# Two long convolutions' last products: own PSUM banks for their third and fourth stage, spare places for late loads and shuffles, additions shared out anew, statistics held back

## The chip, the core and the metric

The kernel runs on one core of a Trainium2 chip. Its engines are TensorE (PE: matmuls), ScalarE (ACT), VectorE (DVE), GpSimd (POOL) and SyncE (SP, which issues DMAs). Each engine takes its instructions in program order; semaphores tie the engines together. PSUM has banks of 2 KB for each of 128 partitions; matmuls write there. The metric is the device time of one execution in microseconds (us).

## The reference

```python
x = A_x                                          # 1 x 2048 x 640, f32
x = x + attention(layernorm(x))                  # 32 heads of 20
x = x + conv(layernorm(x))                       # state space, below
x = x + attention(layernorm(x))
x = x + conv(layernorm(x))

def conv(u, ...):
    K = 2 * real(einsum("dn,dnl->dl", C, exp(A * dt * pos)))
    y = irfft(rfft(u.T, 2 * L) * rfft(K, 2 * L), 2 * L)[:, :L]
    return y.T + u * D_skip
```

The convolution of 640 channels over 2048 positions is done as a Fourier transform, a product with the transformed kernel K, and the transform back.

## The kernel before

The four layers run one after the other: attention 1 (to about 1240 us of the profile), convolution 1 (1259 to 1404), attention 2 (to about 2446, then its output projection), convolution 2 (2493 to 2641, then the last output's DMA). "Conv 1" and "conv 2" stand for the two calls of `ssm`; only the second has `last=True`.

`ssm` is one loop over n = 0 to 54. Channels are in 5 blocks b of 128 (NCT), positions in 16 tiles of 128 (NI). Each block needs eight steps of every stage, so 40 products in all (NQ), and one n holds, in this order: at every fourth n the four spectra `psx` of four products (`sets`, 48 matmuls into four banks F0 to F3); a transpose `pst` (`stage2a`); the loads of product n-2 (`factors`); the sum `x<-x,psy` of the round before; product n-4 (`product`); the first stage of the next block (`stage1`, none from n=32 on); the bn_stats of the round before, for the next layer's norm, in conv 1 only; third stage n-6 (`stage3`: 8 matmuls into `psv`, two ACT copies `v<-psv`); fourth stage n-14 (`stage4`: 8 matmuls into `psy`, of block b and pair i2 of position tiles). `psy` needs the whole `v` of its block. Product k is named by its number 0 to 39, `psy(3,2)` is block 3, i2=2.

One product is four instructions: DVE's shuffle `t<-psx`, DVE's `ka<-psx,ka`, POOL's `kb<-t,kb` and POOL's `ka<-ka,kb`; for k=37 and 39 DVE does the last two too (`alone`). `ka` and `kb` are loaded by SP's DMAs, 256 KB each; `kb` has three buffers (pool `s3`), `t` has one (pool `s4`).

`at` writes the order out by hand: on each engine every instruction of the loop stands behind the one that the code gave it before, so the order of the code is the order of the engine. At the seam between conv 1 and attention 2 a scheduler places what isn't tied. Recorded through a helper, most operations have line 78.

Of the eight banks two belong to pool X, four to F, two to pool M. The two of M (tag `mm`) are shared by `psv`, `psy` and some of stage 1 (`psx1`); the allocator gives a new tile one of the two. Attention 2 begins with the norm: rs and nb of four position tiles (`rstd`), xn on ACT, a transpose `pst`, its split xh and xl, weights wb from DMAs b0s and b1s, then the product `pq`.

Of the kernel before, what the change touches and what calls it, by code (L numbers as in the profile page):

```python
# [11 lines left out]
F32 = mybir.dt.float32  # L12
# [9 lines left out]
P = 128  # L22
L = 2048
D = 640
NI = L // P
NCT = D // P
# [61 lines left out]
def mha_s4d_kernel(ctx, tc, x_in, wqkv, wo, lar, aim, cr, ci, ldt, dsk,  # L88
# [19 lines left out]
    def psum(c, **pools):  # L108
        for n, b in pools.items():
            ps_[n] = c.enter_context(tc.tile_pool(name="ps" + n, bufs=b, space=PSUM))  # L110

    def pst(pool, *a, **k):
        return ps_[pool].tile(*a, **k)
# [7 lines left out]
    ks = dram.tile([2, D, L], F16, name="ks")  # L121
# [65 lines left out]
    last = [None]  # L187
# [1207 lines left out]
    def ssm(x, uh, ul, consts, last):  # L1395
# [19 lines left out]
        with ExitStack() as c:  # L1415
            c1 = c.enter_context(tc.tile_pool(name="s1", bufs=1))
            if last:
                cx = c.enter_context(tc.tile_pool(name="sx", bufs=2))
            c4 = c.enter_context(tc.tile_pool(name="s4", bufs=1))
            c2 = c.enter_context(tc.tile_pool(name="s2", bufs=2))  # L1420
            c3 = c.enter_context(tc.tile_pool(name="s3", bufs=3))
            if not last:
                cx = c2
# [5 lines left out]
            def mm(*a, **k):  # L1429
                at("pe", te.matmul(*a, **k))  # L1430
# [3 lines left out]
            def stage1(b, x1, i2):  # L1434
                bs = slice(b * P, b * P + P)
                spare = b == 1 and i2 in (1, 3, 5) or not b and i2 % 4 > 1 and not last
                pool, tag = ("M", "mm") if spare else ("X", "X")
                ps = pst(pool, [P, 2, 2, P], F32, tag=tag, name="psx1")
                for i in range(2):
                    s = 2 * i2 + i  # L1440
                    for r in range(2):
                        for n, (e, m) in enumerate(((0, uh), (0, ul), (1, uh))):
                            mm(ps[:, r, i, :], e1[:, e, s, r, :], m[:, s, bs], start=(n == 0), stop=(n == 2))
                src = ps.rearrange("p r i (c g) -> p (r i) c g", c=4)
                at("act", se.copy(by_channel(x1[0], i2), src))
                return lambda: at("dve", ve.tensor_sub(by_channel(x1[1], i2), src, by_channel(x1[0], i2)))
# [17 lines left out]

            def factors(m, ch):
                ka = c4.tile([P, 512], F32, bufs=5, name="ka")
                kb = c3.tile([P, 512], F32, name="kb")
                for t, src in ((ka, kha), (kb, khb)):
                    at("sp", sy.dma_start(t.rearrange("p (q k) -> p q k", k=P), src[m][:, ch]))
                return ka, kb  # L1470

            def product(px, ka, kb, alone):
                t2 = c4.tile([P, 512], F32, name="t2")
                at("dve", ve.stream_shuffle(t2, px, SWAP))
                at("dve", ve.tensor_mul(ka, px, ka))
                for f, *a in (("tensor_mul", kb, t2, kb), ("tensor_add", ka, ka, kb)):
                    if alone:
                        at("dve", getattr(ve, f)(*a))
                    else:
                        at("pool", getattr(ge, f)(*a))  # L1480
                return ka

            def stage3(v, t, ch, t1):
                pv = pst("M", [P, 4, 2, NI, 4], F32, tag="mm", name="psv")
                for q in range(4):
                    mm(pv[:, q].rearrange("p r i g -> p (r i g)"), t1[:, q * P:q * P + P], fa, start=True, stop=True)
                for r in range(2):
                    at("act", se.copy(v[:, r, :, ch, 16 * t:16 * t + 16].rearrange("p i (q g) -> p i q g", g=4),
                                      pv[:, :, r].rearrange("p q i g -> p i q g")))

            def stage4(b, v, i2):
                bs, s2 = slice(b * P, b * P + P), slice(2 * i2, 2 * i2 + 2)
                py = pst("M", [P, 2, P], F32, tag="mm", name="psy")
                for i in range(2):
                    for r in range(2):
                        mm(py[:, i, :], eb[:, 2 * i2 + i, r, :], v[:, r, 2 * i2 + i].rearrange("p c g -> p (c g)"),
                           start=(r == 0), stop=(r == 1))

                def add():
                    at("dve", ve.tensor_add(x[:, s2, bs], x[:, s2, bs], py))  # L1500

                def after():
                    if last:
                        if i2 % 2:
                            s4 = slice(2 * i2 - 2, 2 * i2 + 2)
                            at("sp", sy.dma_start(ov[:, s4, bs], x[:, s4, bs]))
                    elif b < NCT - 1:
                        for i in (2 * i2, 2 * i2 + 1):
                            at("dve", ve.bn_stats(st[:, i, b, :], x[:, i, bs]))
                    elif i2 == 1:  # L1510
                        final(0)
                return add, after
# [4 lines left out]
            x1 = new_x1()  # L1517
            for i2 in range(8):
                stage1(0, x1, i2)()
            ks, t1s, vs = {}, {}, {}  # L1520
            NQ = 8 * NCT
            nxt, px = None, None
            sums = None
            for n in range(NQ + 15):
                b, q = divmod(n, 8)
                if n % 4 == 0 and 4 <= n <= NQ:
                    px = sets(xt)
                if n < NQ:
                    if q == 0 and b:
                        x1 = nxt  # L1530
                    if n % 4 == 0:
                        xt = c4.tile([P, 2, 4, 4, P], F16, name="xt")
                    stage2a(x1, q, xt)
                if 2 <= n < NQ + 2:
                    ks[n - 2] = factors(*divmod(n - 2, 4))
                if sums:
                    sums[0]()
                if 4 <= n < NQ + 4:
                    t1s[n - 4] = product(px[n % 4], *ks.pop(n - 4), n > NQ and n % 2 == 1)
                if n < NQ and b + 1 < NCT:  # L1540
                    if q == 0:
                        nxt = new_x1()
                    stage1(b + 1, nxt, q)()
                if sums:
                    sums[1]()
                    sums = None
                if 6 <= n < NQ + 6:
                    m, ch = divmod(n - 6, 4)
                    if m % 2 == 0 and ch == 0:
                        vs[m // 2] = c2.tile([P, 2, NI, 4, 32], F32, name="v")  # L1550
                    stage3(vs[m // 2], m % 2, ch, t1s.pop(n - 6))
                if 14 <= n < NQ + 14:
                    bb, i2 = divmod(n - 14, 8)
                    sums = stage4(bb, vs[bb], i2)
# [93 lines left out]
    def seq(x, general):  # L1648

        stats = None  # L1650
        for n in range(0, len(parts), 2):
            with ExitStack() as c:
# [8 lines left out]
                c3 = ExitStack()  # L1661
# [35 lines left out]
                if not general:  # L1697
                    wc.close()
                c3.close()
                psum(c, M=2, F=1)  # L1700
                end = n + 2 >= len(parts)
                stats = ssm(x, uh, ul, consts, end)
            if early:
# [90 lines left out]
```

## Time and profile before

| | us |
|---|---|
| median of 3 runs | 2644.64 |
| lowest, highest | 2643.77, 2650.95 |
| profiled execution, its span | 2647.0 |
| PE busy | 2492.4 (94%) |
| ACT busy | 2344.0 (89%) |
| DVE busy | 1519.5 (57%) |
| POOL busy | 801.7 (30%) |

For the profiled execution the span from its first to its last instruction is the only time given; it is 2.4 us above the median. The mean granted clock of PE is 0.994. In a timeline a row gives the start, the length from first to last instruction of the row, the instructions, and in brackets how long the engine had been idle and what released it. Rows without a bracket followed with no idle time that counts. Matmuls are pipelined, so a group's length overlaps the next one's; the distance of two starts is what a group costs.

### The profile page before, as it was taken

Reading aid. Unit: us, or ns where it says so; the run is one execution under the profiler, and the core shown is the slowest. Engines: PE = TensorE matmul, PEld = TensorE weight load, DVE = VectorE, ACT = ScalarE, POOL = GpSimd, SP = SyncE. Lnnn points to the kernel's source line nnn. Section 1 sums busy time; section 2 is a strip of 40 time slices with the busy share of each in tenths; the row PEclk is TensorE's granted clock in tenths of the full one; section 3 lists DMA queues with packets and bytes.
Section 4 is the critical chain, followed back from the end, with each engine's and each line's share of the span. In section 5 each row is a group of like instructions: output and inputs, shape, how many; then the busy total and the mean of one; then the engine's idle time right before and its main releaser. Section 6 shows DMA issues by size and latency. Waiting matters only on the chain.

```text
span 2647.0 us, 118800 instructions
## 1 busy us (share of the span) xinstructions
PE 2492.4 (94%) x52388; PEld 1409.8 (53%) x52388; DVE 1519.5 (57%) x3430; ACT 2344.0 (89%) x2763; POOL 801.7 (30%) x1230
## 2 busy tenths in 40 slices
PE   6899999999999999899898999999999998999898
PEld 3444444454444444587896544454444443444898
DVE  7587777777765887577786323232232222143875
ACT  7899999999999999655665899999999999999574
POOL 1123333233323332111681122222222223222285
PEclk9999999999999999999999999999999999999999
DMA  6522222322222221654652111121121113222466
GB/s 206 189 53 77 68 74 62 82 65 63 61 54 59 53 63 38 234 206 163 213 173 64 47 53 50 51 60 45 45 66 39 50 34 87 71 66 61 137 190 184
DMA packets 188158, 241.99 MB, mean 91 GB/s; under 512 B 43504, under 2 KB 128816, under 8 KB 186224
## 3 DMA queue, kind: packets, MB, share of 16 engines
q1 hardware_dynamic: 151936, 188.28, 22.6%
q0 software_dynamic: 35696, 46.01, 7.4%
q8 instruction: 413, 6.77, 1.1%
q14 instruction: 113, 0.93, 0.1%
HBM read 158.16 MB, written 76.00 MB: 88 GB/s over the span
## 4 chain that ended last, share of the span: by engine, by line
ACT 59%; PE 20%; issue 10%; DVE 3%; DMA 2%; POOL 1%; SPq 0%; ACTq 0%; POOLq 0%; DVEq 0%
ACT pt L78 57%; PE psy L1430 3%; PE pa L903 2%; PE psv L1430 2%; PE po L193 2%; PE psx L1430 2%; PE S L868 2%; PE pst L1452 1%; PE pkx L193 1%; PE pv L586 1%; PE m L620 1%; PE pkt L196 1%; PE pq L773 1%; DMA kb<-khb 1%; DMA kop<-ks 1%
## 5 line engine op out<-in xcount | busy, mean ns | idle before, releaser
L78 ACT ACTIVATE pt<-S 128x1024 f32<-128x1024 f32 x2048 | 1927.7, 1033 | 27.9 <-PE S L868 15.5
L903 PE MATMUL pa<-pt,V 64*32 64x512 f32 x16384 | 1096.9, 589 | 1.4 <-DVE oc L78 1.4
L868 PE MATMUL S<-qop,kop 61*32 61x512 f16 x16384 | 877.2, 380 | 82.7 <-ACT pt L78 67.8
L868 PEld LDWEIGHTS <-kop 61*32 61x32 f16 x16384 | 366.9, 89 | 737.3 <-issue 619.2
L903 PEld LDWEIGHTS pa<-pt,V 64*32 64x32 f32 x16384 | 312.7, 106 | 72.0 <-issue 8.6
L78 POOL DMA_DIRECT2D dn<-oc x248 | 122.7, 501 | 574.2 <-DVE oc L78 574.1
L78 DVE TENSOR_SCALAR qc<-m 128x512 f32<-128x512 f32 (+1 forms) x68 | 46.8, 688 | 312.0 <-PE m L620 312.0
L78 POOL DMA_DIRECT2D db<-dn x248 | 125.4, 512 | 141.5 <-DMA dn<-dr 136.9
L78 POOL DMA_DIRECT2D ot<-oc x256 | 130.5, 517 | 88.4 <-DVE oc L78 55.5
L620 PE MATMUL m<-xl,wh 64*32 64x512 f16 x2560 | 143.8, 376 | 0.3 <-issue 0.3
L620 PE MATMUL m<-xh,wh 64*32 64x512 f16 x2560 | 144.1, 378 | 0.0
L620 PE MATMUL m<-xh,wl 64*32 64x512 f16 x2560 | 143.8, 377 | 0.0
L78 DVE COPY oc<-pa 128x512 f32<-128x512 f32 x64 | 44.2, 690 | 172.9 <-PE pa L903 168.9
L78 ACT COPY xt<-pst 128x1024 f16<-128x1024 f16 x80 | 81.3, 1016 | 60.8 <-PE pst L1452 60.8
L620 PEld LDWEIGHTS <-wh 64*32 64x32 f16 x5120 | 90.3, 93 | 73.3 <-issue 30.8
L78 POOL DMA_DIRECT2D dn<-dr x62 | 34.6, 558 | 287.3 <-DVE dr L78 248.6
L1480 POOL TENSOR_TENSOR kb<-t,kb 128x512 f32<-128x512 f32 x76 | 97.2, 1280 | 65.2 <-DVE t L78 40.8
L78 DVE TENSOR_SCALAR V<-m 128x160 f32<-128x160 f32 x64 | 20.7, 324 | 163.4 <-PE m L586 163.4
L78 DVE TENSOR_TENSOR kb<-ktab 128x512 f32<-128x512 f32 x160 | 106.2, 683 | 0.0
L586 PEld LDWEIGHTS <-xh 128*128 128x128 f16 x960 | 79.7, 98 | 46.7 <-issue 31.4
L1480 POOL TENSOR_TENSOR ka<-ka,kb 128x512 f32<-128x512 f32 x76 | 97.5, 1283 | 6.0
L337 PEld LDWEIGHTS m<-kb,ka 128*32 128x32 f32 x3840 | 60.8, 109 | 71.0 <-issue 52.4
(312 smaller groups left out, 3936.4 us busy)
## 6 DMA issues: line engine op xcount, KB each, us to landing
ka<-kha SPq DMA_DIRECT2D x80, 256.0 KB
kb<-khb SPq DMA_DIRECT2D x80, 256.0 KB
db<-dn POOLq DMA_DIRECT2D x248, 64.0 KB, 3.2
kop<-ks SPq DMA_DIRECT2D x176, 80.0 KB
kpw<-wd POOLq DMA_DIRECT2D x60, 192.0 KB, 3.9
qop<-qs SPq DMA_DIRECT2D x256, 40.0 KB
ot<-oc POOLq DMA_DIRECT2D x256, 40.0 KB, 3.0
kha<-kn SPq DMA_DIRECT2D x20, 512.0 KB
```

Source lines behind the costliest of these rows:

```text
L78: made = f(out, *a, **k)
L193: chain(te.matmul(*a, **k))
L196: chain(te.transpose(*a, **k))
L337: chain(te.matmul(ps[32 * j:32 * j + 32, c8, :], a[n][:, ch, :], b[n][:, dd, :], start=(n == 0), stop=(n == 2), tile_position=(0, 32 * j)))
L586: chain(te.matmul(ps[:, :n], a_[:, ct, sl], m[:, ct, :], start=(k == 0), stop=(k == 14)))
L620: chain(te.matmul(ps[r][32 * t:32 * t + 32, :], a_[rows, ct, 32 * u:32 * u + 32], m[rows, ct, 512 * v:512 * v + 512], start=(k == 0), stop ...
L773: te.matmul(pq, a_[:, ct, :], m[:, ct, sl], start=(n == 0), stop=(n == 14))
L868: chain(te.matmul(S[32 * t:32 * t + 32, 512 * r:512 * r + 512], kt_[rows, kc + 32 * t:kc + 32 * t + 32], qt[rows, :], start=True, stop=Tru ...
L903: chain(te.matmul(pa[r][32 * j:32 * j + 32, :], V[rows, kt, VP * h:VP * h + 32], pts[j // 2][rows, 512 * (j % 2):512 * (j % 2) + 512], sta ...
L1430: at("pe", te.matmul(*a, **k))
L1452: at("pe", te.transpose(pt[:, k, g, :], of_group(x1[k], 4 * q + g), id16))
L1480: at("pool", getattr(ge, f)(*a))
```

## The change

Pool M goes; pools V and Y get one bank each. `psv` lives in V, `psy` in Y, but the `psy` of block 4 with odd i2 in V; the spare `psx1` take V or Y.

From n=34 on the two buffers of the first stage's `x1` are not used any more; they are taken over as `room0`, four places for the shuffled spectra of products 32 to 39, and `room1`, four places for the kb loads of the same products.

POOL's and DVE's shares of products change: k=37 goes back to POOL whole, k=38 goes to DVE whole, and of k=33, 35 and 39 DVE does the addition alone. Of the 16 POOL-kind operations of k=32 to 39 DVE had 4 and has 5.

In conv 1 the bn_stats of the rounds n-1=40 to 45 (block 3, i2 = 2 to 7: 12 instructions) are held and issued one pair a round at n=49 to 54.

```diff
--- before.py
+++ after.py
@@ -1434,8 +1434,8 @@
             def stage1(b, x1, i2):
                 bs = slice(b * P, b * P + P)
                 spare = b == 1 and i2 in (1, 3, 5) or not b and i2 % 4 > 1 and not last
-                pool, tag = ("M", "mm") if spare else ("X", "X")
-                ps = pst(pool, [P, 2, 2, P], F32, tag=tag, name="psx1")
+                pool = ("Y" if b or i2 % 2 else "V") if spare else "X"
+                ps = pst(pool, [P, 2, 2, P], F32, tag=pool, name="psx1")
                 for i in range(2):
                     s = 2 * i2 + i
                     for r in range(2):
@@ -1464,24 +1464,24 @@
 
             def factors(m, ch):
                 ka = c4.tile([P, 512], F32, bufs=5, name="ka")
-                kb = c3.tile([P, 512], F32, name="kb")
+                kb = room[1][:, ch] if m >= 2 * NCT - 2 else c3.tile([P, 512], F32, name="kb")
                 for t, src in ((ka, kha), (kb, khb)):
                     at("sp", sy.dma_start(t.rearrange("p (q k) -> p q k", k=P), src[m][:, ch]))
                 return ka, kb
 
-            def product(px, ka, kb, alone):
-                t2 = c4.tile([P, 512], F32, name="t2")
+            def product(px, ka, kb, k):
+                t2 = room[0][:, k % 4] if k >= NQ - 8 else c4.tile([P, 512], F32, name="t2")
                 at("dve", ve.stream_shuffle(t2, px, SWAP))
                 at("dve", ve.tensor_mul(ka, px, ka))
                 for f, *a in (("tensor_mul", kb, t2, kb), ("tensor_add", ka, ka, kb)):
-                    if alone:
+                    if k == NQ - 2 or f == "tensor_add" and (k == NQ - 1 or k in (NQ - 7, NQ - 5)):
                         at("dve", getattr(ve, f)(*a))
                     else:
                         at("pool", getattr(ge, f)(*a))
                 return ka
 
             def stage3(v, t, ch, t1):
-                pv = pst("M", [P, 4, 2, NI, 4], F32, tag="mm", name="psv")
+                pv = pst("V", [P, 4, 2, NI, 4], F32, tag="V", name="psv")
                 for q in range(4):
                     mm(pv[:, q].rearrange("p r i g -> p (r i g)"), t1[:, q * P:q * P + P], fa, start=True, stop=True)
                 for r in range(2):
@@ -1489,8 +1489,9 @@
                                       pv[:, :, r].rearrange("p q i g -> p i q g")))
 
             def stage4(b, v, i2):
+                pool = "V" if b == NCT - 1 and i2 % 2 else "Y"
                 bs, s2 = slice(b * P, b * P + P), slice(2 * i2, 2 * i2 + 2)
-                py = pst("M", [P, 2, P], F32, tag="mm", name="psy")
+                py = pst(pool, [P, 2, P], F32, tag=pool, name="psy")
                 for i in range(2):
                     for r in range(2):
                         mm(py[:, i, :], eb[:, 2 * i2 + i, r, :], v[:, r, 2 * i2 + i].rearrange("p c g -> p (c g)"),
@@ -1520,9 +1521,11 @@
             ks, t1s, vs = {}, {}, {}
             NQ = 8 * NCT
             nxt, px = None, None
-            sums = None
+            sums, held = None, []
             for n in range(NQ + 15):
                 b, q = divmod(n, 8)
+                if n == NQ - 6:
+                    room = [cx.tile([P, 4, 512], F32, tag=f"x1{k}", name=f"room{k}") for k in range(2)]
                 if n % 4 == 0 and 4 <= n <= NQ:
                     px = sets(xt)
                 if n < NQ:
@@ -1536,14 +1539,16 @@
                 if sums:
                     sums[0]()
                 if 4 <= n < NQ + 4:
-                    t1s[n - 4] = product(px[n % 4], *ks.pop(n - 4), n > NQ and n % 2 == 1)
+                    t1s[n - 4] = product(px[n % 4], *ks.pop(n - 4), n - 4)
                 if n < NQ and b + 1 < NCT:
                     if q == 0:
                         nxt = new_x1()
                     stage1(b + 1, nxt, q)()
                 if sums:
-                    sums[1]()
+                    (held.append if not last and NQ <= n - 1 < NQ + 6 else lambda f: f())(sums[1])
                     sums = None
+                if held and n > NQ + 8:
+                    held.pop(0)()
                 if 6 <= n < NQ + 6:
                     m, ch = divmod(n - 6, 4)
                     if m % 2 == 0 and ch == 0:
@@ -1697,7 +1702,7 @@
                 if not general:
                     wc.close()
                 c3.close()
-                psum(c, M=2, F=1)
+                psum(c, V=1, Y=1, F=1)
                 end = n + 2 >= len(parts)
                 stats = ssm(x, uh, ul, consts, end)
             if early:
```

DVE at the end of conv 1, before: the sum of `psy`, the shuffle, the product and the statistics of k=33 and k=34.

```order
L78 TENSOR_TENSOR x<-x,psy 128x2x128 [waits PE_49]
L78 STREAM_SHUFFLE t_31085<-psx_30984 128x512 [waits Pool_49]
L78 TENSOR_TENSOR ka<-psx_30984,ka 128x512 [waits DMAHW6_49]
L78 BN_STATS st_28889<-x 128x6 [waits DVE_49]
L78 BN_STATS st_28889<-x 128x6
L78 TENSOR_TENSOR x<-x,psy 128x2x128 [waits PE_49]
L78 STREAM_SHUFFLE t_31119<-psx_30985 128x512 [waits Pool_49]
L78 TENSOR_TENSOR ka<-psx_30985,ka 128x512 [waits DMAHW0_49]
L78 BN_STATS st_28889<-x 128x6 [waits DVE_49]
L78 BN_STATS st_28889<-x 128x6
```

DVE at the same place now; `room_30918` is the place of the shuffles, `room_30919` that of the kb loads.

```order
L78 TENSOR_TENSOR x<-x,psy 128x2x128 [waits PE_49]
L78 STREAM_SHUFFLE room_30918<-psx_30987 128x512
L78 TENSOR_TENSOR ka<-psx_30987,ka 128x512 [waits DMAHW6_49]
L78 TENSOR_TENSOR ka<-ka,room_30919 128x512 [waits DMAHW7_49,DVE_49,Pool_49]
L78 BN_STATS st_28892<-x 128x6 x2
L78 TENSOR_TENSOR x<-x,psy 128x2x128 [waits PE_49]
L78 STREAM_SHUFFLE room_30918<-psx_30988 128x512
L78 TENSOR_TENSOR ka<-psx_30988,ka 128x512 [waits DMAHW0_49]
L78 BN_STATS st_28892<-x 128x6 [waits DVE_49]
L78 BN_STATS st_28892<-x 128x6
```

The addition of k=33 has come in ahead of the statistics and of the next sum of `psy`, and it waits for POOL; the shuffles no longer wait for POOL.

POOL at the end of conv 1, products 33 to 36, before.

```order
L1480 TENSOR_TENSOR kb<-t_31051,kb 128x512 [waits DMAHW5_49,DVE_49]
L1480 TENSOR_TENSOR ka<-ka,kb 128x512 [waits DVE_49,DMAHW4_49,PE_49,Pool_49]
L1480 TENSOR_TENSOR kb<-t_31085,kb 128x512 [waits DMAHW7_49,DVE_49]
L1480 TENSOR_TENSOR ka<-ka,kb 128x512 [waits DVE_49,DMAHW6_49,PE_49,Pool_49]
L1480 TENSOR_TENSOR kb<-t_31119,kb 128x512 [waits DMAHW1_49,DVE_49]
L1480 TENSOR_TENSOR ka<-ka,kb 128x512 [waits DVE_49,DMAHW0_49,PE_49,Pool_49]
L1480 TENSOR_TENSOR kb<-t_31154,kb 128x512 [waits DMAHW3_49,DVE_49]
L1480 TENSOR_TENSOR ka<-ka,kb 128x512 [waits DVE_49,DMAHW2_49,PE_49,Pool_49]
```

POOL at the same place now, products 33 to 37.

```order
L1480 TENSOR_TENSOR room_30919<-room_30918,room_30919 128x512 [waits DMAHW5_49,DVE_49]
L1480 TENSOR_TENSOR ka<-ka,room_30919 128x512 [waits DVE_49,DMAHW4_49,PE_49,Pool_49]
L1480 TENSOR_TENSOR room_30919<-room_30918,room_30919 128x512 [waits DMAHW7_49,DVE_49]
L1480 TENSOR_TENSOR room_30919<-room_30918,room_30919 128x512 [waits DMAHW1_49,DVE_49]
L1480 TENSOR_TENSOR ka<-ka,room_30919 128x512 [waits DVE_49,DMAHW0_49,PE_49,Pool_49]
L1480 TENSOR_TENSOR room_30919<-room_30918,room_30919 128x512 [waits DMAHW3_49,DVE_49]
L1480 TENSOR_TENSOR room_30919<-room_30918,room_30919 128x512 [waits DMAHW5_49,DVE_49]
L1480 TENSOR_TENSOR ka<-ka,room_30919 128x512 [waits DVE_49,DMAHW4_49,PE_49,Pool_49]
```

The additions of k=33 and 35 are gone from POOL, so it goes from one kb product to the next one; each of these waits for a shuffle of DVE.

PE at the end of conv 1 before, from `psv` of k=36 and `psy(3,4)` on.

```order
L1430 MATMUL psv<-fa,ka 128x128 [waits PE_49,DMAHW4_49,Activation_49,Pool_49]
L1430 MATMUL psv<-fa,ka 128x128 x3
L1430 MATMUL psy<-v,eb 128x128 [waits PE_49,Activation_49]
L1430 MATMUL psy<-v,eb 128x128 x3
L1430 MATMUL psv<-fa,ka 128x128 [waits DMAHW6_49,DVE_49]
L1430 MATMUL psv<-fa,ka 128x128 x3
L1430 MATMUL psy<-v,eb 128x128 [waits PE_49,Activation_49]
L1430 MATMUL psy<-v,eb 128x128 x3
```

PE at the same place now.

```order
L1430 MATMUL psv<-fa,ka 128x128 [waits PE_49,DMAHW4_49,Activation_49,Pool_49]
L1430 MATMUL psv<-fa,ka 128x128 x3
L1430 MATMUL psy<-v,eb 128x128 [waits DVE_49]
L1430 MATMUL psy<-v,eb 128x128 x3
L1430 MATMUL psv<-fa,ka 128x128 [waits PE_49,DMAHW6_49,Activation_49,Pool_49]
L1430 MATMUL psv<-fa,ka 128x128 x3
L1430 MATMUL psy<-v,eb 128x128 [waits DVE_49]
L1430 MATMUL psy<-v,eb 128x128 x3
```

`psy` waited for ACT, which empties the `psv` just written; it now waits for DVE, which empties the `psy` of the round before.

## Rows read from the trace of the kernel before

**Rows 1.** The page, part 4: the chain that ended last, by engine.
```profile
ACT 59%; PE 20%; issue 10%; DVE 3%; DMA 2%; POOL 1%; SPq 0%; ACTq 0%; POOLq 0%; DVEq 0%
```

**Rows 2.** Timeline, PE, end of conv 1: start us, us, instructions [idle before <-releaser].
```profile
1374.61 1.11 PE L1430 MATMUL psv<-fa,ka 128*128 128x128 f32 x8
1375.56 1.06 PE L1430 MATMUL psy<-v,eb 128*128 128x128 f32 x8
...
1385.99 1.16 PE L1430 MATMUL psv<-fa,ka 128*128 128x128 f32 x8
1387.89 1.16 PE L1430 MATMUL psy<-v,eb 128*128 128x128 f32 x8 [0.73 <-ACT v L78]
...
1395.35 8.43 PE L1430 MATMUL psy<-v,eb 128*128 128x128 f32 x72
```

**Rows 3.** Timeline, ACT, end of conv 1.
```profile
1387.19 0.65 ACT L78 COPY v<-psv 128x256 f32<-128x256 f32 x2 [1.31 <-PE psv L1430]
```

**Rows 4.** Timeline, DVE, end of conv 1.
```profile
1376.65 0.42 DVE L78 TENSOR_TENSOR x<-x,psy 128x256 f32<-128x256 f32 x1 [0.30 <-PE psy L1430]
...
1384.63 0.74 DVE L78 STREAM_SHUFFLE t<-psx 128x512 f32<-128x512 f32 x1
1385.26 0.67 DVE L78 TENSOR_TENSOR ka<-psx,ka 128x512 f32<-128x512 f32 x1
1385.85 0.68 DVE L78 TENSOR_TENSOR kb<-t,kb 128x512 f32<-128x512 f32 x1
1386.57 0.69 DVE L78 TENSOR_TENSOR ka<-ka,kb 128x512 f32<-128x512 f32 x1
1387.18 0.48 DVE L78 BATCH_NORM_STATS2 st<-x 128x6 f32<-128x128 f32 x2
1387.57 0.40 DVE L78 TENSOR_TENSOR x<-x,psy 128x256 f32<-128x256 f32 x1
```

**Rows 5.** Timeline, POOL, end of conv 1.
```profile
1375.53 1.29 POOL L1480 TENSOR_TENSOR kb<-t,kb 128x512 f32<-128x512 f32 x1
1376.90 1.27 POOL L1480 TENSOR_TENSOR ka<-ka,kb 128x512 f32<-128x512 f32 x1
...
1384.66 1.28 POOL L1480 TENSOR_TENSOR ka<-ka,kb 128x512 f32<-128x512 f32 x1
```

**Rows 6.** Timeline, PE, end of conv 2.
```profile
2623.45 1.16 PE L1430 MATMUL psv<-fa,ka 128*128 128x128 f32 x8 [0.52 <-POOL ka L1480]
...
2628.47 1.16 PE L1430 MATMUL psv<-fa,ka 128*128 128x128 f32 x8 [0.18 <-POOL ka L1480]
...
2632.25 8.31 PE L1430 MATMUL psy<-v,eb 128*128 128x128 f32 x72
```

**Rows 7.** Timeline, POOL, end of conv 2.
```profile
2618.19 1.28 POOL L1480 TENSOR_TENSOR kb<-t,kb 128x512 f32<-128x512 f32 x1 [0.56 <-DMA kb<-khb]
```

**Rows 8.** Timeline, DVE, the projection ahead of conv 2.
```profile
2489.04 1.17 DVE L78 TENSOR_TENSOR lt<-rs 128x2 f32<-128x2 f32 x1
2490.24 0.16 DVE L78 TENSOR_TENSOR lt<-lt,va 128x2 f32<-128x2 f32 x1
```

**Rows 9.** Timeline, POOL, the same stretch.
```profile
2480.82 1.42 POOL L1236 TENSOR_TENSOR ulx<-u,uhx 128x640 f16<-128x640 f32 x1 [0.17 <-ACT uhx L78]
2486.82 3.37 POOL L1236 TENSOR_TENSOR ulx<-u,uhx 128x640 f16<-128x640 f32 x2 [4.59 <-ACT uhx L78]
```

**Rows 10.** Timeline, DVE, start of attention 2.
```profile
1407.29 0.82 DVE L78 TENSOR_REDUCE wm<-b0s 128x1 f32<-128x640 f32 x1 [0.46 <-DMA b0s<-in_wqkv]
...
1410.79 3.13 DVE L78 TENSOR_TENSOR xl<-pst,xh 128x512 f16<-128x512 f32 x5
```

**Rows 11.** Timeline, PE, start of attention 2.
```profile
1411.53 0.66 PE L823 MATMUL pst<-ident,xn 128*128 128x128 f32 x4 [3.51 <-DVE xl L78]
```

**Rows 12.** Busy us by window of attention 2's start (window, us, engines, PEclk, DMA, GB/s).
```profile
core 0: us, PE busy (x) PEld busy (x) DVE busy (x) ACT busy (x) POOL busy (x), PEclk, DMA share, GB/s
...
1412.00:1416.00 4.00, 4.00 (x13) 1.45 (x12) 3.71 (x6) 3.64 (x6) 0.00 (x0) 0.57 0.22 71
1416.00:1420.00 4.00, 4.00 (x20) 1.83 (x19) 2.69 (x11) 1.40 (x5) 0.00 (x0) 1.00 0.11 35
```

## The prediction

> **What bounds the kernel now.** I began with the chain that ended last: 59% ACT, the exponentials of attention, which this change leaves alone, and 20% PE [rows 1]. So the timelines of the two convolutions' ends come next, where the diff acts, PE's first, since the loop ends with its last `psy`. While there are transposes to do, PE goes without a pause: `psv` and `psy` start 0.95 apart, and the sum on DVE starts 1.09 after its `psy` and is done 0.42 later [rows 2, 4]. In the last rounds PE waits. In conv 1 the wait is for a bank: `psv` of k=36 starts at 1385.99, ACT copies it from 1387.19 for 0.65, and only then, at 1387.89, does `psy(3,4)` start: 1.90 from start to start instead of 0.95 [rows 2, 3]. There are three such pairs (k=36, 37, 38), so 3 x 0.95 = 2.85 us. In conv 2 there are two (k=36, 38), and two waits for POOL's `ka`, of 0.52 and 0.18 [rows 6]: 2 x 0.95 + 0.70 = 2.6 us. 5.5 us in all is what this end has to give, 0.2% of the time.
>
> The next view is POOL. A product takes it from 1375.53 to 1376.90 and on to the next, 2.6 us, and runs so back to back to the addition that starts at 1384.66 [rows 5]; DVE's parts of a product lie between those. In this stretch POOL sets when `ka` is there, and DVE has some air.
>
> **Separate banks.** By the order of the changed kernel, `psy` no longer waits for the `psv` just written. The 0.95 of each pair goes. What stands in its place: a `psy` needs its own bank empty, which by the rows is 1.09 + 0.42 + 0.05 = 1.56 us after the start of the `psy` before it (the 0.05 is the way from ACT's copy, ended at 1387.84, to PE's start at 1387.89 [rows 2, 3]). That is hidden while a `psv` lies between (0.95 + 0.89 = 1.84), provided DVE comes to the sum at once. It isn't hidden at `psy(4,0)`, which follows `psy(3,7)` directly: 1.56 - 0.89 = 0.67 us of new wait in each conv, where before 72 matmuls ran through in 8.43 us [rows 2]. After that, block 4 alternates between two banks and nothing waits. In the earlier rounds a transpose and stage 1 lie between, so I cost the split at nothing there; the cover is PE's own work.
>
> **Places for loads and shuffles.** Shuffles no longer wait for POOL's product to free `t`; the loads of k=35 to 39 no longer wait for a third `kb`. The one place where that shows is conv 2: POOL waits 0.56 us for `kb` of k=35 [rows 7]. Gone, it lets POOL start that product at the same time as before, no earlier, because of the next point.
>
> **Sums shared out anew: k=33 and 35.** This I replayed by hand with the order's waits and the rows' durations: on DVE shuffle 0.63, product 0.59, kb product 0.72, addition 0.61, statistics 0.39 from start to start [rows 4]; on POOL 1.36 and 1.24 [rows 5]. The same replay of the kernel before gives every start of PE in conv 1 within 0.2 us, up to `psy(3,7)`.
> - Conv 1: POOL's product of k=33 runs 1375.53 to 1376.82 as before [rows 5]. DVE, free at 1375.88, must wait for it: its addition starts at 1376.87, a stall of 1.0. Behind it in DVE's queue stand the statistics, the sum of `psy(2,7)` and shuffle 34. The sum comes at 1377.87 instead of 1376.65 [rows 4], so `psy(3,0)` is 0.4 later; the shuffle lets POOL, idle since 1376.82, start product 34 at 1379.02 instead of 1378.13. DVE and POOL now take turns where they overlapped. At k=35 the same costs DVE 1.6 us, and `psy(3,2)` starts at 1384.43 instead of 1383.12. `psv` of k=36 starts at 1387.80 against 1385.99 [rows 2].
> - From there the three bank waits are gone; in their place `psv` of k=37 waits 0.76 for POOL, which now has all of k=37, `psy(3,6)` waits 0.68 behind the addition of k=39, and `psy(4,0)` its 0.67. `psy(3,7)` starts at 1395.77 against 1395.35, `psy(4,0)` at 1397.33 against 1395.35 + 0.89 = 1396.24 [rows 2]: **+1.1 us**.
> - Conv 2, without statistics and with POOL later against PE: `psv` of k=36 at 2623.88 against 2623.45, the same waits behind it, `psy(4,0)` at 2633.30 against 2632.25 + 0.89 = 2633.14 [rows 6]: **+0.1 us**, rounded down.
>
> **k=38 whole on DVE.** Here lies a cost that the end of the kernel before doesn't show. DVE's two instructions of k=38 read two tiles from SBUF each, and by the replay they fall on POOL's product and addition of k=37. Before, DVE's pair started at 1385.85 just as POOL's addition ended (1384.66 + 1.28 = 1385.94 [rows 4, 5]), so it met no POOL work. The nearest rows are in the projection ahead of conv 2: DVE's `lt<-rs`, two tiny SBUF inputs, took 1.17 us instead of 0.16 and ended at 2490.21, with POOL's `ulx`, which ran until 2490.19; and POOL's pair of `ulx` took 3.37 instead of 2 x 1.42 = 2.84 [rows 8, 9]. So the one stands still until the other is done. In the replay DVE's product of k=38 comes first at 1389.03, POOL's addition then waits to 1389.71 and runs to 1390.99, and DVE's addition waits for that: it is done at 1391.6 instead of 1390.36. The sum for Y, shuffle 39, POOL's product of 39 and DVE's addition follow in a row, and `psy(3,6)` and all behind it are 1.25 later. Bounds: 0 (no collision) and 1.25 per conv; I take 1.25, as the rows show a full stop, in both: **+2.5 us**.
>
> The Trainium skill, "SBUF — State Buffer", section "SBUF: two separate sides", says that VectorE with two SBUF inputs and a GpSimd operation that reads SBUF lock each other out for a whole instruction. By that rule the term is the 2.5 above, and were the two sides of SBUF free of each other it would be 0 and the sum 2646.4. The trace agrees with the rule, as 2490.21 against 2490.19 shows.
>
> **Statistics later, and the seam.** Six pairs of 0.39 us leave DVE's tight rounds in conv 1; this is in the replay. They return between the last sums and attention 2's weights. After conv 1's last `psy`, DVE waits 0.46 for b0s, and `xl` starts at 1410.79, which ends PE's wait of 3.51 [rows 10, 11]. By the new order the held statistics fill those waits, and two aggregations and a statistic come between b1s and `wb`: 0.75 us, less the cast `sel`, 0.17, that now lies ahead: `xl` **+0.6 us**. Bounds -0.5 and +3. The norm of the second four tiles comes late, behind the first queries' squares; PE has the values `pv` of the first tiles to do meanwhile, so I cost it at nothing; without this cover it is a rival below.
>
> **Sum.** +1.1 + 0.1 + 2.5 + 0.6 = +4.3 us. The profiled span of 2647.0 is 2.4 above the median of the runs; the differences carry over, so 2644.6 + 4.3 = **2648.9 us**. About 0.3% (7.9 us) is what a measurement of this kernel tells from no change; the three runs lie 7.2 apart.
>
> **Rivals.**
> - No collision at k=38 (DVE and POOL fall past each other, or the lock is shorter): 2648.9 - 2.5 = 2646.4. For it: a shift of DVE by one instruction is enough. Against it: POOL has 2.6 us of work there without a gap.
> - The waits go as the change has it: DVE's additions find POOL done, so all 5.5 us of waits at the two ends vanish, and only the seam costs: 2644.6 - 5.5 + 0.6 = 2639.7. For it: DVE has fewer statistics in conv 1, loads and shuffles come early. Against it: POOL's product of k=33 can't start earlier than POOL's addition of k=32 ends, and DVE stands there before.
> - Slower: at the seam PE has nothing between the first queries and the late second norm. It would stand still a second time, up to 3.5 us as in rows 11. Its granted clock was 0.57 in the 4 us after that first wait and 1.00 after [rows 12], that is mostly at 1.2 GHz instead of 2.4, so 0.43 x 4 = 1.7 us more: 2648.9 + 5.2 = 2654.1. It decides at whether `pv` of the first tiles is ready when the first queries end.
> - The change does nothing that counts, since waits of one kind replace another: 2644.6.
>
> **How the numbers follow.** Forecast 0.42, no collision 0.24, waits vanish 0.15, slower 0.12, nothing 0.07. The range reaches from 2640, which leaves out half of the third case, to 2653, which leaves out most of the fourth. Faster by over 0.3% is below 2636.7, which only the third case with the seam's gain nears: 0.04. Slower by over 0.3% is above 2652.6: most of the fourth case, 0.11. Within: 0.85.
>
> **What would show it.** Right: DVE idle about 1.0 and 1.6 us ahead of the additions of k=33 and 35, released by POOL; `psy` after `psv` without ACT's wait; PE idle 0.67 ahead of `psy(4,0)`; DVE's or POOL's instructions of k=37 and 38 at twice their length, ending together; `xl` 7.6 us after the last `psy`'s end instead of 7.0. Wrong: PE without idle from k=36 on, or a second stop of PE in the first 20 us of attention 2.

## The result, and the profile after

| | changed | before |
|---|---|---|
| median of 22 runs each, us | 2651.58 | 2645.86 |
| lowest to highest, us | 2645.71 to 2656.63 | 2641.40 to 2652.91 |
| profiled execution, span, us | 2650.4 | 2647.0 |

The ratio to the kernel before is 1.0022, with a 95% interval of 1.0015 to 1.0028: 4.0 to 7.4 us more. The forecast was 4.3 more, 2648.9 us; the measured median is 2.7 above that and inside the range. Of these 2.7 us 1.2 are the starting point (the kernel before has 2645.86 in 22 runs, 2644.64 in the three that the forecast started from) and 1.4 the change itself (5.7 against 4.3).

Where it went is read from PE first. A measure that attention's own scatter doesn't touch is the stretch from the spectra of n=36 to the start of `psy(4,0)`. Where no row begins with `psy(4,0)`, its start is that of `psy(3,7)` plus 0.89. Ahead of this stretch the new banks cost nothing: from a conv's first `sets` (n=4) to that of n=36 it took 94.63 and 94.54 us before, 94.49 and 94.56 after. Before: 1370.86 to 1395.35 + 0.89, that is 25.38 us in conv 1, and 2607.70 to 2632.25 + 0.89, 25.44 us, in conv 2. PE in the changed kernel, conv 1, a timeline:

```profile
1370.63 0.92 PE L1430 MATMUL psx<-xt,f2s 32*32 32x512 f16 x48
...
1378.09 1.16 PE L1430 MATMUL psy<-v,eb 128*128 128x128 f32 x8 [0.23 <-DVE x L78]
...
1384.16 1.16 PE L1430 MATMUL psy<-v,eb 128*128 128x128 f32 x8 [0.64 <-DVE x L78]
...
1387.51 1.16 PE L1430 MATMUL psv<-fa,ka 128*128 128x128 f32 x8 [0.26 <-POOL ka L1480]
...
1390.09 1.16 PE L1430 MATMUL psv<-fa,ka 128*128 128x128 f32 x8 [0.53 <-POOL ka L1480]
1391.70 1.16 PE L1430 MATMUL psy<-v,eb 128*128 128x128 f32 x8 [0.45 <-DVE x L78]
...
1394.76 1.16 PE L1430 MATMUL psy<-v,eb 128*128 128x128 f32 x8 [1.01 <-DVE x L78]
...
1396.64 1.06 PE L1430 MATMUL psy<-v,eb 128*128 128x128 f32 x8
1398.31 7.53 PE L1430 MATMUL psy<-v,eb 128*128 128x128 f32 x64 [0.60 <-DVE x L78]
```

From 1370.63 to 1398.31 is 27.68 us: 2.30 more. The waits of rows 2 for ACT are gone. In their place stand waits for the sum on DVE ("DVE x") and for POOL's `ka`, and 0.60 ahead of `psy(4,0)`. DVE and POOL at the same place, the instructions of k=33, 35, 37, 38 and 39:

```profile
1376.62 0.69 DVE L78 TENSOR_TENSOR ka<-ka,room 128x512 f32<-128x512 f32 x1 [0.89 <-POOL room L1480]
...
1382.70 0.69 DVE L78 TENSOR_TENSOR ka<-ka,room 128x512 f32<-128x512 f32 x1 [1.49 <-POOL room L1480]
...
1388.27 0.67 DVE L78 TENSOR_TENSOR ka<-psx,ka 128x512 f32<-128x512 f32 x1
1388.86 1.73 DVE L78 TENSOR_TENSOR room<-room,room 128x512 f32<-128x512 f32 x1
1390.62 0.69 DVE L78 TENSOR_TENSOR ka<-ka,room 128x512 f32<-128x512 f32 x1
...
1393.68 0.69 DVE L78 TENSOR_TENSOR ka<-ka,room 128x512 f32<-128x512 f32 x1 [0.81 <-POOL room L1480]
```

```profile
1375.30 1.29 POOL L1480 TENSOR_TENSOR room<-room,room 128x512 f32<-128x512 f32 x1
1378.77 1.30 POOL L1480 TENSOR_TENSOR room<-room,room 128x512 f32<-128x512 f32 x1 [2.18 <-DVE room L78]
...
1384.84 1.27 POOL L1480 TENSOR_TENSOR room<-room,room 128x512 f32<-128x512 f32 x1 [2.17 <-DVE room L78]
...
1387.41 1.28 POOL L1480 TENSOR_TENSOR room<-room,room 128x512 f32<-128x512 f32 x1
1388.77 1.27 POOL L1480 TENSOR_TENSOR ka<-ka,room 128x512 f32<-128x512 f32 x1
```

DVE stands 0.89 and 1.49 us until POOL's products of k=33 and 35 are there, and POOL, which ran without a gap before [rows 5], stands 2.18 and 2.17 until DVE comes to the next shuffle: they take turns. At 1388.86 DVE's product of k=38 takes 1.73 us, where the row of before (k=37's product, on DVE) has 0.68 [rows 4]; POOL's addition of k=37 runs from 1388.77 to 1390.04, and DVE is done 0.55 after that. The instruction ahead of it, `ka<-psx,ka`, has one of its inputs in PSUM: it runs beside POOL's product (1387.41 to 1388.69) and takes its usual 0.67.

Conv 2, PE, and then DVE and POOL at k=37 and 38:

```profile
2609.95 0.92 PE L1430 MATMUL psx<-xt,f2s 32*32 32x512 f16 x48
...
2626.04 1.16 PE L1430 MATMUL psv<-fa,ka 128*128 128x128 f32 x8 [0.43 <-POOL ka L1480]
...
2629.06 1.16 PE L1430 MATMUL psv<-fa,ka 128*128 128x128 f32 x8 [0.97 <-POOL ka L1480]
...
2633.01 1.16 PE L1430 MATMUL psy<-v,eb 128*128 128x128 f32 x8 [0.89 <-DVE x L78]
...
2636.56 7.38 PE L1430 MATMUL psy<-v,eb 128*128 128x128 f32 x64 [0.61 <-DVE x L78]
```

```profile
2627.21 0.68 DVE L78 TENSOR_TENSOR room<-room,room 128x512 f32<-128x512 f32 x1
2627.92 1.64 DVE L78 TENSOR_TENSOR ka<-ka,room 128x512 f32<-128x512 f32 x1
```

```profile
2625.94 1.28 POOL L1480 TENSOR_TENSOR room<-room,room 128x512 f32<-128x512 f32 x1
2627.29 1.72 POOL L1480 TENSOR_TENSOR ka<-ka,room 128x512 f32<-128x512 f32 x1
```

From 2609.95 to 2636.56 is 26.61 us, 1.17 more than before. Here DVE's product came first, at 2627.21, and the two instructions that follow are both stretched: POOL's addition to 1.72, DVE's to 1.64.

At the seam, DVE and PE of the changed kernel:

```profile
1409.31 0.82 DVE L78 TENSOR_REDUCE wm<-b0s 128x1 f32<-128x640 f32 x1 [0.39 <-DMA b0s<-in_wqkv]
...
1413.29 3.07 DVE L78 TENSOR_TENSOR xl<-pst,xh 128x512 f16<-128x512 f32 x5
```

```profile
1423.71 0.55 PE L823 MATMUL pst<-ident,xn 128*128 128x128 f32 x3 [0.34 <-ACT xn L78]
...
1440.32 0.66 PE L823 MATMUL pst<-ident,xn 128*128 128x128 f32 x4 [0.77 <-DVE xl L78]
```

`xl` begins 7.45 us after the end of the last `psy` (1398.31 + 7.53 = 1405.84), 7.01 before [rows 10]. DVE's wait for b0s, which the held statistics were to fill, is still 0.39, against 0.46. PE then waits twice more, 0.34 and 0.77. In the kernel before it waits twice in that stretch too, but for others and less:

```profile
1421.95 0.66 PE L823 MATMUL pst<-ident,xn 128*128 128x128 f32 x4 [0.19 <-ACT qc L78]
...
1433.11 0.30 PE L586 MATMUL pv<-wv,xh 128*128 128x160 f16 x2 [0.20 <-DVE V L78]
```

### The profile page after: what moved, and what is told of

Read it like the earlier page. It is cut to its first block, busy times and chain, and to the rows that moved or that the text cites. A ratio compares the mean times of both kernels' runs of the same rounds, so it can differ in the third digit from the quotient of the medians.

```text
span 2650.4 us, 118792 instructions
## 1 busy us (share of the span) xinstructions
PE 2494.5 (94%) x52388; PEld 1411.4 (53%) x52388; DVE 1521.8 (57%) x3432; ACT 2342.8 (88%) x2763; POOL 799.5 (30%) x1228
## 5 line engine op out<-in xcount | busy, mean ns | idle before, releaser
L1480 POOL TENSOR_TENSOR kb<-t,kb 128x512 f32<-128x512 f32 x64 | 81.8, 1279 | 59.9 <-DVE t L78 59.5
L1430 PE MATMUL psv<-fa,ka 128*128 128x128 f32 x640 | 88.9, 282 | 2.2 <-POOL ka L1480 2.2
```

## The experiments

The theory: the new shares make DVE and POOL wait for each other, at k=33, 35 and 38, and that is nearly all of the loss; the statistics cost a little at the seam. The main rival: the single banks, which tie `psy` to DVE's sum, cost it. Edits are against the changed kernel where nothing else is said. "Stretch" is the measure above, conv 1 and conv 2.

| kernel | stretches, us | ratio to before |
|---|---|---|
| before | 25.38, 25.44 | |
| changed | 27.68, 26.61 | 1.0022 (1.0015 to 1.0028) |
| old shares | 25.24, 25.25 | 1.0006 (0.9998 to 1.0015) |
| before + new shares | 26.87, 26.85 | 1.0010 (1.0002 to 1.0019) |
| additions of k=33, 35 back | 25.92, 25.91 | |
| k=38 back on POOL | 27.85, 27.08 | |
| POOL's k=37 only writes | 26.62, 25.69 | |
| statistics back | 28.41, 26.61 | |
| banks of block 4 turned | 26.85, 25.82 | |
| turned, shares with k=38 alone | 24.51, 24.56 | 0.9993 (0.9984 to 1.0001) |
| the same, statistics back | 24.93, 24.53 | 0.9996 (0.9987 to 1.0004) |
| shared banks back | 26.93, 26.57 | |
| before + held statistics | 24.81, 25.86 | 1.0001 (0.9993 to 1.0010) |
| places back | 27.73, 27.31 | |

A stretch is read from one execution. Kernels whose conv 2 has the same code agree to 0.03 with the spare places (26.61 and 26.61; 24.56 and 24.53); without them 25.44 and 25.86 differ by 0.42. Where no ratio stands, the kernel ran once, and its whole time is not used.

### Old shares

```diff
-if k == NQ - 2 or f == "tensor_add" and (k == NQ - 1 or k in (NQ - 7, NQ - 5)):
+if k in (NQ - 3, NQ - 1):
```

> The changed kernel with the old shares: DVE does both last steps of k=37 and 39, POOL the rest; banks, places and held statistics stay changed. Measure: PE from the spectra of n=36 to psy(4,0), 25.38 us in conv 1 and 25.44 in conv 2 before, 27.68 and 26.61 after. Theory (the new shares cost it all): about 25.4 and 25.1, so 3.8 us under the changed kernel, and of the time before only the seam's 0.2 to 0.4 us is left; ratio to before 0.999 to 1.001. Rival (the single banks cost it, above all psy waiting for the sum on DVE): both stretches stay above 26.3 and the ratio is 1.001 to 1.002.

Measured: 25.24 and 25.25, ratio 1.0006. The loss at both ends goes with the shares, as the theory has it. With the old shares the banks, places and statistics give the two ends 0.14 and 0.19 us: what the bank waits of before gave up is taken again by waits for DVE, as its PE rows in conv 1 show:

```profile
1386.53 1.16 PE L1430 MATMUL psy<-v,eb 128*128 128x128 f32 x8 [0.45 <-DVE x L78]
...
1389.89 1.16 PE L1430 MATMUL psv<-fa,ka 128*128 128x128 f32 x8 [0.42 <-POOL ka L1480]
1391.50 1.16 PE L1430 MATMUL psy<-v,eb 128*128 128x128 f32 x8 [0.45 <-DVE x L78]
...
1395.05 7.53 PE L1430 MATMUL psy<-v,eb 128*128 128x128 f32 x64 [0.61 <-DVE x L78]
```

0.45, 0.42, 0.45 and 0.61 in place of 0.73, 0.74 and 0.74. The collision isn't gone with the new shares: DVE, no longer held up at its shuffles, now comes to its product of k=39 while POOL adds k=38, and takes 1.09 in both convs (1389.29 in conv 1) in place of 0.68.

### New shares alone

```diff
 (against the kernel before)
-if alone:
+if k == NQ - 2 or f == "tensor_add" and (k == NQ - 1 or k in (NQ - 7, NQ - 5)):
```

> The kernel before with the new shares alone (k=38 whole on DVE, the additions of k=33, 35 and 39 on DVE). Theory: DVE stands 0.9 and 1.5 us ahead of the additions of k=33 and 35 and the pair of k=38 is stretched by POOL, with the old banks too: 27.2 in conv 1 (25.38 + 1.8) and 25.9 in conv 2, 2.3 us over the time before, ratio 1.0005 to 1.0015. Rival (the banks cost it): 25.4 in both, ratio 1.000.

Measured: 26.87 and 26.85, 1.5 and 1.4 over before, ratio 1.0010. The shares cost by themselves, with the old banks too. Two points missed. Conv 2 lost 0.9 more than expected, with POOL 0.73 late for `kb` of k=35 (0.56 in the kernel before), which the replay had left out; up to 0.4 of it can be scatter. And nothing was stretched: with one buffer `t`, shuffle 38 waits until POOL's product of k=37 is done, so DVE comes to its pair as POOL ends.

```profile
2626.05 0.69 DVE L78 TENSOR_TENSOR kb<-t,kb 128x512 f32<-128x512 f32 x1
2626.77 0.69 DVE L78 TENSOR_TENSOR ka<-ka,kb 128x512 f32<-128x512 f32 x1
```

```profile
2617.90 1.27 POOL L1480 TENSOR_TENSOR kb<-t,kb 128x512 f32<-128x512 f32 x1 [0.73 <-DMA kb<-khb]
...
2624.87 1.27 POOL L1480 TENSOR_TENSOR ka<-ka,kb 128x512 f32<-128x512 f32 x1
```

POOL's addition of k=37 ends at 2626.14, DVE's product starts at 2626.05 and takes 0.69. So this collision needs the spare places as well.

### The additions of k=33 and 35 back on POOL

```diff
-if k == NQ - 2 or f == "tensor_add" and (k == NQ - 1 or k in (NQ - 7, NQ - 5)):
+if k == NQ - 2 or f == "tensor_add" and k == NQ - 1:
```

> The changed kernel with the additions of k=33 and 35 back on POOL; k=38 stays whole on DVE, the addition of k=39 too. Theory (these waits take their own share): DVE goes on without a stop at k=33 and 35, conv 1 falls by 1.7 to 26.0, conv 2 by 0.9 to 25.7. Rival (the collision at k=38 is the whole loss): 27.7 and 26.6 stay.

Measured: 25.92 and 25.91, 1.76 and 0.70 less. Not all of that is the two waits, since the collision is shorter here:

```profile
1387.40 1.37 DVE L78 TENSOR_TENSOR room<-room,room 128x512 f32<-128x512 f32 x1
```

DVE comes to its product of k=38 16.82 us after the spectra of n=36 in both convs (1387.40 - 1370.58 in conv 1), against 18.23 and 17.26 in the changed kernel: the waits are 1.41 and 0.44. The rest, 0.35 and 0.26, is the collision, 1.37 and 1.36 long in place of 1.73 and 1.64. So in conv 1 the two waits are the larger part of the loss; in conv 2 they aren't.

### k=38 back on POOL, and POOL's k=37 without reading

```diff
-if k == NQ - 2 or f == "tensor_add" and (k == NQ - 1 or k in (NQ - 7, NQ - 5)):
+if f == "tensor_add" and (k == NQ - 1 or k in (NQ - 7, NQ - 5)):
```

> The changed kernel with k=38 whole on POOL; the additions of k=33, 35 and 39 stay on DVE. No DVE instruction with two SBUF inputs then meets POOL at k=37 and 38. If the collision by itself costs 1.25 us a conv, as the prediction's sum has it: 26.4 in conv 1 and 25.4 in conv 2. By a replay with POOL's added 2.6 us in it: POOL's own work takes the place of the collision, 27.8 and 26.7, no gain.

```diff
+if k == NQ - 3:
+    at("pool", ge.memset(a[0], 0.0))
-if k == NQ - 2 or f == "tensor_add" and (k == NQ - 1 or k in (NQ - 7, NQ - 5)):
+elif k == NQ - 2 or f == "tensor_add" and (k == NQ - 1 or k in (NQ - 7, NQ - 5)):
```

> The changed kernel with POOL's two steps of k=37 replaced by memsets of the same two tiles (product 37 is left out, so its part of the output is missing): POOL is busy at that place, but reads nothing. Theory (the two of DVE and POOL that read SBUF shut each other out): DVE's pair of k=38 takes 0.68 and 0.69 us, not 1.73 or 1.64 for one of them, and the stretch from the spectra of n=36 to psy(4,0) falls by 1.3 us in each conv, to 26.4 and 25.3. Rival (any POOL work beside it, or DVE's wait for something else): one of the pair stays above 1.2 us and the stretches stay.

Measured: with k=38 on POOL 27.85 and 27.08, nothing gained, and 0.47 lost in conv 2; with memsets 26.62 and 25.69, 1.06 and 0.92 less. PE, DVE and POOL of the second, conv 1:

```profile
1372.55 0.92 PE L1430 MATMUL psx<-xt,f2s 32*32 32x512 f16 x48
...
1390.76 0.68 DVE L78 TENSOR_TENSOR room<-room,room 128x512 f32<-128x512 f32 x1
1391.48 0.69 DVE L78 TENSOR_TENSOR ka<-ka,room 128x512 f32<-128x512 f32 x1
```

```profile
1388.10 1.27 POOL L1482 TENSOR_TENSOR ka<-ka,room 128x512 f32<-128x512 f32 x1
1389.32 0.52 POOL L78 MEMSET room<- 128x512 f32 x1
1389.78 0.52 POOL L78 MEMSET ka<- 128x512 f32 x1
```

The pair is back to 0.68 and 0.69. The memsets are over by 1390.30, before the pair starts, so this run doesn't tell a POOL that writes from a POOL that is idle. What it does tell is the price. DVE comes to the pair as late as in the changed kernel, 18.21 us after the spectra of n=36 (1390.76 - 1372.55) against 18.23 (1388.86 - 1370.63), and is through with it 1.06 earlier; the stretch falls by the same 1.06. So the collision costs 1.06 in conv 1 and 0.92 in conv 2. With the 1.41 and 0.44 of the waits that is 2.47 and 1.36, against the 2.44 and 1.36 that the old shares gave back (where a collision of 1.09 is left at k=39). The other run says that the price can't be won by handing k=38 to POOL: then DVE stands 2.62 us for POOL ahead of the addition of k=39, and the end waits for POOL instead. What the addition of k=39 costs by being on DVE was not tried by itself; DVE stands 0.81 ahead of it in the changed kernel.

### Statistics, held and not

```diff
-(held.append if not last and NQ <= n - 1 < NQ + 6 else lambda f: f())(sums[1])
+sums[1]()
```

> The changed kernel with the statistics at their old place. Theory: conv 1's stretch grows by 0.8 us to 28.5, since the statistics stand in DVE's queue between the addition and the sum that psy waits for; xl starts 7.0 us after the last psy's end as before, not 7.45: 0.4 us back at the seam. Conv 2 has none and stays at 26.6. Rival (holding them back is worth nothing in conv 1): 27.7 stays, and the whole 0.4 is won.

The same part alone was put into the kernel before:

> The kernel before with conv 1's statistics of block 3 held back, nothing else. Theory: conv 1's stretch stays 25.4, since DVE has room there with the old shares; the first exponential of attention 2 comes 0.6 to 1.3 us later after the last psy (66.4 to 67.1, not 65.5), ratio 1.0000 to 1.0005. Rival (the statistics fall into DVE's idle time at the seam): 65.5 and ratio 1.000.

Measured without holding: conv 1 28.41, 0.73 more; conv 2 26.61 again; `xl` 6.89 after the end of the last `psy`. Holding alone, in the kernel before: 24.81, 0.57 less than 25.38, which the theory had as no change. In that program `psy(3,5)` no longer waits for ACT, so it got the other of the two shared banks; of the three waits of rows 2 (0.73, 0.74, 0.74) two are left, with 0.16 for POOL. The 0.74 less 0.16 that this gives is the whole gain: the allocator's choice, not room on DVE. Conv 2, whose code is as before, has 25.86 there, with POOL standing 1.05 ahead of its product of k=35, not 0.56. At the seam PE shows the price, in the kernel with held statistics alone and then in the changed one with them put back:

```profile
1415.28 0.55 PE L823 MATMUL pst<-ident,xn 128*128 128x128 f32 x3 [0.34 <-ACT xn L78]
...
1431.89 0.66 PE L823 MATMUL pst<-ident,xn 128*128 128x128 f32 x4 [0.77 <-DVE xl L78]
```

```profile
1425.78 0.66 PE L823 MATMUL pst<-ident,xn 128*128 128x128 f32 x4 [0.19 <-ACT qc L78]
...
1436.94 0.30 PE L586 MATMUL pv<-wv,xh 128*128 128x160 f16 x2 [0.20 <-DVE V L78]
```

0.34 and 0.77 against 0.19 and 0.20: the second norm comes late, and so does the split `xl` of the tiles after it. The ten kernels that hold all have these two waits (0.34 or 0.35, 0.76 or 0.77), the four that don't all have the other two (0.19, 0.20 or 0.21). Added to the 0.44 of `xl` that is 0.72 + 0.44 = 1.2 us. From the end of conv 1's last `psy` to the first exponential of attention 2 it took 66.8 us in the mean of the ten (65.0 to 68.1) and 65.6 in the mean of the four (64.8 to 66.2). The delay lasts: to the spectra of n=36 in conv 2 it took 1204.6 in the mean of the ten and 1203.2 in the mean of the four. The gain at the end of conv 1, 0.73 here and 0.42 in the last pair of versions below, is less than that; the ratio of the held statistics alone, 1.0001, can't tell.

### The banks

```diff
-pool = "V" if b == NCT - 1 and i2 % 2 else "Y"
+pool = "V" if b == NCT - 1 and i2 % 2 == 0 else "Y"
```

> The changed kernel with the banks of block 4 turned about: psy(4,0) goes to V, whose copies it awaits anyway, and psy(4,1) to Y. Theory: the wait of 0.60 ahead of psy(4,0) goes, both stretches fall by 0.6 us, to 27.1 and 26.0. Rival (psy(4,0) then waits as long for ACT's copies of k=39): 27.7 and 26.6 stay.

Measured: 26.85 and 25.82, 0.83 and 0.79 less, more than the idle time of 0.60: from start to start `psy(3,7)` cost 1.67 us (1396.64 to 1398.31) where 0.89 is usual, and this 0.78 is what goes. `psy(4,0)` in V runs straight on:

```profile
1391.05 8.46 PE L1430 MATMUL psy<-v,eb 128*128 128x128 f32 x72
```

The other way round, pool M with its two shared banks again for `psv`, `psy` and the spare `psx1`:

> The changed kernel with the shared pool of two banks for psv, psy and spare psx1. Theory (with the new shares DVE's lateness sets PE's pace, the bank hardly does): conv 1 27.5 to 27.8, conv 2 25.6 to 26.2, as psy(4,0) needs no wait of its own but pairs with psv do. Rival (the split is what costs): both at 26 or less.

Measured: 26.93 and 26.57. In conv 1 0.75 less, in conv 2 the same: the theory's 27.5 to 27.8 and 25.6 to 26.2 missed on both sides. The split with the parity that the change gave it costs conv 1 0.75 us under the new shares, about what turning the banks brings. So the rival has a part, a third of conv 1's 2.30, but only together with the new shares: with the old ones the same split costs nothing (25.24 against 25.38).

### The places back

```diff
-kb = room[1][:, ch] if m >= 2 * NCT - 2 else c3.tile([P, 512], F32, name="kb")
+kb = c3.tile([P, 512], F32, name="kb")
-t2 = room[0][:, k % 4] if k >= NQ - 8 else c4.tile([P, 512], F32, name="t2")
+t2 = c4.tile([P, 512], F32, name="t2")
 (the two lines that allocate room go too)
```

> The changed kernel without the spare places: one buffer for the shuffles, three for the kb loads. Theory (POOL and DVE take turns at k=33 and 35 anyway, so a free place lets nothing start sooner): both stretches within 0.2 us of 27.68 and 26.61, in conv 2 up to 0.5 more where POOL waits for kb of k=35. Rival (the places make up for part of the loss): 1 us more in each.

Measured: 27.73 and 27.31. Nothing in conv 1, 0.70 in conv 2, where POOL stands 0.32 us ahead of its product of k=35, which it doesn't in the changed kernel. The pair of k=38 isn't stretched here either (0.68 and 0.69 in conv 1), and yet conv 1's stretch is as long: without places DVE waits for POOL ahead of shuffle 38, with them inside the pair.

### Versions meant to beat both

Turned banks, and of the shares only k=38 whole on DVE:

```diff
-if k == NQ - 2 or f == "tensor_add" and (k == NQ - 1 or k in (NQ - 7, NQ - 5)):
+if k == NQ - 2:
-pool = "V" if b == NCT - 1 and i2 % 2 else "Y"
+pool = "V" if b == NCT - 1 and i2 % 2 == 0 else "Y"
```

> A version meant to beat both: the changed kernel with turned banks (psy(4,0) in V) and with POOL doing all but k=38, which DVE does whole. By the replay 24.8 us in each conv, 0.6 under the kernel before in each, with 0.2 to 0.4 us lost at the seam: 0.8 us under the time before, ratio 0.9995 to 1.000, hardly to be told from it; against the changed kernel 5 us less. Rival (the banks themselves cost): above 25.5 in both, ratio over 1.0005.

> The version of turned banks and k=38 alone on DVE, with the statistics at their old place as well. Theory (holding them back costs more at the seam than it gives in conv 1's end once the shares don't press DVE): conv 1's stretch grows from 24.51 by 0.4 to 24.9, conv 2 stays 24.56, and the first exponential of attention 2 comes 1.1 us sooner after conv 1's last psy (65.8, not 66.9): 1.4 us under the kernel before, ratio 0.9990 to 0.9998. Rival (the seam is indifferent): 24.9 and a first exponential at 67, so worse than the held version by 0.4.

Measured: 24.51 and 24.56 with held statistics, median 2644.95; 24.93 and 24.53 without, median 2644.11, the first exponential 64.8 us after the last `psy`. The kernel before had 2645.94 and 2645.97 beside them. Both intervals hold 1: the 0.9 us at each end (0.5 in conv 1 without holding) is seen in the trace, the ratio can't confirm it. Against the changed kernel both would be 0.3% better (0.9993 / 1.0022 = 0.9971, 0.9996 / 1.0022 = 0.9974); they didn't run beside it. The collision is still in them. DVE and POOL with held statistics, conv 1:

```profile
1384.54 1.37 DVE L78 TENSOR_TENSOR room<-room,room 128x512 f32<-128x512 f32 x1
```

```profile
1384.09 1.27 POOL L1480 TENSOR_TENSOR ka<-ka,room 128x512 f32<-128x512 f32 x1
```

In conv 2 it is 1.42. By these lengths some 0.7 us more could be won at each end with k=38 at a place where POOL stands still; that is an estimate, no version tried it.

## Why the prediction was right, point by point

- **k=33 and 35.** Forecast: DVE stalls 1.0 and 1.6, `psy(3,2)` late. Measured 0.89 and 1.49, released by POOL. Undone, 1.76 and 0.70 us come back, of which 1.41 and 0.44 are these waits. In conv 2 the stalls are 0.86 and 1.75. Right in place and size.
- **Separate banks.** Forecast: 0.95 of each pair goes, 0.67 ahead of `psy(4,0)` comes. Measured: no wait for ACT left, 0.60 and 0.61 idle ahead of `psy(4,0)`, 0.78 from start to start; turned banks take it away. Right.
- **k=38 on DVE.** Forecast: a full stop, DVE's product first, then POOL's addition, then DVE's, 1.25 per conv. Measured: so in conv 2; in conv 1 POOL's addition was first by 0.09, and only DVE's product was stretched. The stretched ones took 1.73 and 1.64 for 0.68, and they didn't end together with POOL's but 0.55 later. The mechanism was right, the order in conv 1 was not, and the price, 1.06 and 0.92, is less than the 1.25.
- **The two ends.** 1.1 + 1.25 = 2.35 in conv 1 and 0.1 + 1.25 = 1.35 in conv 2, against 2.30 and 1.17. That they come so near is in part luck: without the collision the ends lose 1.24 and 0.25 (26.62 and 25.69 against before), more than the 1.1 and 0.1, and the collision costs less than its 1.25; the two errors cancel.
- **Places.** Costed at nothing in conv 1: 0.05 measured. In conv 2 they save 0.70 where the forecast gave them none, and had POOL's wait of 0.56 for k=35 [rows 7] go without use.
- **The seam.** 0.6 forecast, about 1.2 measured. `xl` moved 0.44, though DVE's wait for b0s was hardly filled; the mis-sized part is the late second norm, costed at nothing under the cover of `pv`: the cover holds but for 0.34 + 0.77 - 0.19 - 0.20 = 0.72 us. The slower rival was this mechanism at five times its size: between its wait for the first `xl` (2.41) and the first scores, PE's longest wait is 0.77, not 3.5.
- **The sum.** 2.30 + 1.17 + 1.16 = 4.6 us is located, inside the 4.0 to 7.4 of the runs; the medians differ by 5.7. In the profiled pair the seam doesn't show: its spans differ by 3.4, which is no more than the two ends. What the other 1.1 is stays open. Single spans of attention scatter by more: the spectra of n=36 in conv 1 start between 1365.1 and 1372.6 in the fourteen profiles. The mean granted clock of PE is 0.9931 in the 22 runs of the changed kernel and 0.9940 in the 63 runs of the kernel before beside the experiments; whether part of the 1.1 lies there was not tried. The rival that all waits vanish fell with the first rows of after, that of no collision with the 1.73.

## What to carry to other kernels

Work that two in-order engines shared was here best handed over in whole pieces (k=38 alone on DVE: 24.51 and 24.56 with turned banks, against 26.85 and 25.82 with the additions too): an instruction that waits for the other engine holds up all behind it, here a sum that frees a bank and a shuffle that the other engine waits for, and overlap turns into taking turns. A resource made free (a bank, a buffer) pays only what the next wait leaves: write down who empties it and what stands ahead of that in its queue. Replaying a few rounds of four queues by hand, with starts from the trace and the new order, gave the two ends within 0.2 us, with errors of 0.1 to 0.3 in the parts; what was costed at nothing by a cover was the part that came out too small. To price a collision, take the other engine's work away and see that the first engine comes to the place at the same time and leaves it earlier.

## What the runs showed of the hardware

DVE's instructions with two SBUF inputs, 0.68 or 0.69 us alone, were stretched beside POOL's addition: the product to 1.73 in conv 1, the addition to 1.64 in conv 2. Both ended 0.55 after POOL's (1390.59 against 1390.04; 2629.56 against 2629.01). So did every pair that was stretched in the other kernels, 0.55 in all, however long the two overlapped: 1.73 us where DVE's began 0.09 behind POOL's, 1.37 where 0.45 (1384.54 and 1384.09 above), 1.09 where 0.73 (1389.29 and 1388.56, old shares). A wait for POOL's end and then the whole 0.68 would end 0.13 later than that. It works both ways: POOL's addition took 1.72 instead of 1.28 where DVE's product was 0.08 ahead, 0.16 less than a full wait would make it. The Trainium skill, "SBUF — State Buffer", section "SBUF: two separate sides", says that whoever starts first holds the shared ports for its whole instruction; the trace agrees with both orders, at 1388.86 and at 2627.21, but for these 0.13 and 0.16. The two sides in that section's title are the engines' ports and the DMA's, not VectorE's and GpSimd's, as the prediction has it where it sets its term to 0.
